# Two of six triangular inverses move to GpSimd, VectorE's work in PSUM, and a new order for the planned part

## The chip, the cores and the metric

The kernel runs on one core of one Trainium2 chip. The metric is device time in microseconds (us) of one execution; the kernel before takes 930.67 us, the median of three runs (928.48 to 932.31). A profile of a single execution is read beside it.

## The reference, cut to what matters

Three layers follow each other. The first is a delta-rule attention over 32 heads (4 batches of 8), 768 steps, head size 48; the second sends each of the 3072 tokens to one of 8 experts; the third is a dense layer with SiLU.

```
for t in range(768):                       # every head
    y[t]  = q[t] @ state
    state = state + beta[t] * outer(k_n[t], v[t] - k_n[t] @ state)
e   = argmax(x @ w_gate + bias[modality])   # x = y, 384 wide
out = gate * (relu(x @ w1[e]) @ w2[e])      # hidden 1024
h   = out @ w_in;  y = (h * sigmoid(h)) @ w_out   # hidden 2048
```

All data are float32. The kernel works on the attention in chunks: within 128 steps the recurrence becomes a lower triangular system, whose inverse is needed before the chunk can touch the state.

## The kernel before, in words

The sequence is cut into six tiles of 128 steps, numbered 0 to 5, each in two halves p of the heads. For one tile TensorE makes Gram matrices of the keys (`gram`, job "gr") and of queries with keys ("gq"); ScalarE copies them to the array `G`, and VectorE masks the second kind into `KB` (`keep_reads`, job "Kc", L347). VectorE turns the 32x32 diagonal blocks into lanes (`to_lanes`, "L", L361), works out scales (`scales`, "b2", L373 to L383), and inverts all of them at once in 31 steps (`step`, "st"): step j scales eight columns of `L` now and then (L399), and adds to the columns right of j of the array `A`, for j under 3 with one instruction a row (L403), later with a product into `tmp` (L416) and a sum into `A` (L422), each split in even and odd rows. `spread` ("sp", L438) turns `A` back into `G`. From there TensorE joins blocks ("px", "pt", "po"), weighs keys ("w"), and goes through the states ("up", "ps", "py"), ScalarE copying every result out of PSUM. Tile t+1's states wait for tile t's. `lengthen` ("ln", L388) and `values` ("va") feed the values.

After tiles 1, 2, 4 and 5 a routing piece ("wv") picks experts for the tokens at hand and makes lists of rows ("idx"). GpSimd gathers rows by these lists ("xg"). Nine expert slots follow: five of 256 tokens (slots 0 to 4), whose work stands in the same plan as the attention, and four of 512 tokens, written as a loop (`regular`). A slot has eight chunks; for each chunk TensorE multiplies nine float32r products ("fi", L1252) and, in the five small slots, two plain float32 products ("se", L1346, four records in a trace). The dense layer follows with six groups of 512 tokens, and its weights are prepared (`Parts64`) on VectorE and ScalarE while the experts run.

What sets the order. `Attention.plan` and `Experts.plan` hand about 1700 jobs with an engine, a cost and predecessors to `Order.solve`, a list scheduler that picks among ready jobs by a rank (a table of numbers, `PLAN["rank"]`, minus the length of the tail). `Order.emit` then writes all jobs in order of planned start, and ties each engine's instructions in that order. So every engine works strictly in its planned order, and each of its waits holds back all that is behind it. Where TensorE has a planned gap of over 0.35 us, `pulses` puts in products of ones with ones (L709, 512 columns), whose results nobody reads; after 0.9 us of gap a pulse waits for the last VectorE or ScalarE job that the plan has just finished. They stop at the time at which the first list of rows is planned to be ready.

Of the kernel before, what the change touches and what calls it, by code (L numbers as in the profile page):

```python
# [7 lines left out]
F32 = mybir.dt.float32  # L8
# [14 lines left out]
    one=3, pair=(),  # L23
    rank=dict(
        kq=198.9, qb=242.4, vs=64.9, kd=1074.8, gr=178.8, gq=-206.4, Gc=265.8, Kc=-543.5, dg=116.5, zero=481.9,
        L=-45.2, sc=-154.7, b2=340.1, ln=213.1, va=184.7, st=-507.6, sp=-287.4, ga=-146.4, px=174.1, pt=-1057.9,
        X=305.7, T=-753.7, po=227.7, o=-75.7, w=-47.4, wc=358.3, up=-972, uc=248.6, ps=313.7, sc2=440.7, py=-130,
        Y=295.3, out=42.8, xt=584.3, xc=262.8, gt=-535.2, wv1=331.6, wv2=-1257.8, wv4=-528.6, wv5=1423.9, one=13,
        kz=-116.7, ask=630.4, gates=494.4, val=-1272.9, fe=560.9, xg=-121.2, tr=351.3, th=-1084.9, tl=-543.8,
        s1h=188.5, s1l=-470.8, fi=62.6, rh=1130.9, se=363.3, ev=879.6, ys=-330, kq0=-992.8, kq1=204, kq2=-239,  # L30
        kq3=1181.7, kq4=1140.9, kq5=361.6, qb0=-834.3, qb1=213, qb2=198.2, qb3=-423.8, qb4=-77.2, qb5=-59.4,
        vs0=275.8, vs1=225.8, vs2=298.3, vs3=263.5, vs4=296.8, vs5=998, kd0=157.9, kd1=428.8, kd2=-1243.7,
        kd3=-217.5, kd4=145.9, kd5=155.3, gr0=-340.2, gr1=-583.9, gr2=-34.8, gr3=329.1, gr4=454.4, gr5=93.2,
        gq0=-633.4, gq1=162.2, gq2=-384.1, gq3=-361, gq4=1032.9, gq5=1017.3, Gc0=235.9, Gc1=-709.5, Gc2=429.7,
        Gc3=314.6, Gc4=-129.9, Gc5=270.9, Kc0=-373, Kc1=999.8, Kc2=144.2, Kc3=-455.6, Kc4=155, Kc5=266.9, dg0=-223.6,
        dg1=-1210.5, dg2=1184.8, dg3=-248, dg4=-20.1, dg5=-606.1, zero0=116.4, zero1=332.4, zero2=1460.5,
        zero3=248.9, zero4=333.9, zero5=159.4, L0=447.7, L1=-430.7, L2=924.8, L3=192.6, L4=921.1, L5=183, sc0=1012.1,
        sc1=-98.1, sc3=224.1, sc4=1211.5, sc5=-69.1, b20=922.8, b21=538.7, b22=973.6, b23=880.2, b24=185.3,
        b25=1234.7, ln0=-63.4, ln1=1192.8, ln2=1025.7, ln3=125.5, ln4=-1285.8, ln5=-18.4, va0=-105.9, va1=173.4,
        va2=-105.7, va3=542.3, va4=-431.2, va5=-166.7, st0=-382.7, st1=226.4, st2=409.7, st3=238.7, st4=991.3,  # L40
        st5=297.4, sp0=1026.6, sp1=-1254, sp2=258.7, sp3=-652.1, sp4=319.6, sp5=-558.9, ga0=216.1, ga1=274.9,
        ga2=-353.3, ga3=81.8, ga4=378.1, ga5=-391.6, px0=-256, px1=-219.1, px2=-501.3, px3=228.8, px4=-782.7,
        px5=-706.1, pt0=1186.1, pt1=1, pt2=1002.2, pt3=-69.1, pt4=137.4, pt5=540.7, X0=154.8, X1=-283.2, X2=143.5,
        X3=223.1, X4=167.8, X5=355.1, T0=-942.6, T1=-981.1, T2=559.4, T3=375.1, T4=290.1, T5=-757.6, po0=-44.5,
        po1=-483.3, po2=37.4, po3=453.9, po4=173.6, po5=7.6, o0=547.1, o1=1388.5, o2=-397.4, o3=-1124.1, o4=-93.5,
        o5=1261.4, w0=607.9, w1=-55.3, w2=250.4, w3=-492.5, w4=338.1, w5=-29.2, wc0=441.5, wc1=204.1, wc2=-303.8,
        wc3=303.5, wc4=18.8, wc5=-839.4, up0=307.4, up1=961.3, up2=997.7, up3=151.7, up4=276.1, up5=165.9, uc0=71.2,
        uc1=7.9, uc2=168.8, uc3=400.9, uc4=-365.6, uc5=-21.5, ps0=-362, ps1=192.1, ps2=-98.2, ps3=-284.9,
        ps4=-1201.7, ps5=388.1, sc20=-17.9, sc21=-203.8, sc22=1135, sc23=1058.3, sc24=266, sc25=262.1, py0=-1236.1,
        py1=-1483.9, py2=178.4, py3=159.7, py4=157.6, py5=260.2, Y0=-591.1, Y1=106.6, Y2=225.6, Y3=173.9, Y4=-364.7,  # L50
        Y5=581.7, out0=1102.9, out1=219.8, out2=-5, out3=1095, out4=106.6, out5=7.9, xt0=-110.6, xt1=1262.9,
        xt2=-77.8, xt3=558.1, xt4=320.5, xt5=-355.9, xc0=-1176.7, xc1=446.2, xc2=190.5, xc3=1185.8, xc4=-1224.2,
        xc5=-108.2, gt0=-51.7, gt1=446.3, gt2=320.9, gt3=-396.2, gt4=195.5, gt5=988.7,
    ), half=82.5,
    ex=300.9, n0=40, npre=40, tok=70,
# [3 lines left out]
class Order:  # L59
# [1803 lines left out]
```

## Time and profile before

| | us |
|---|---|
| device time, median of 3 (lowest, highest) | 930.67 (928.48, 932.31) |
| profiled execution, device time | 937.53 |
| profiled execution, span | 935.8 |
| TensorE busy | 887.8 (95%) |
| VectorE busy | 587.1 (63%) |
| ScalarE busy | 424.6 (45%) |
| GpSimd busy | 80.9 (9%) |
| mean granted TensorE clock | 0.97 of full speed |

The profiled execution takes 6.9 us more than the median of the runs, and its span is 1.7 us shorter than its own device time. TensorE's busy time holds the idle products and counts a product from its start to its modelled end, so it isn't work at the peak. The span has three parts: the planned part up to the last eviction of slot 4, the four large expert slots, and the dense layer. Names of tiles in the rows are the program's: `KKQ` and `KRH` are keys, `bank` the five PSUM banks of the plan, `po` two further ones that hold the experts' sums, `raw` the expert weights as fetched, `wRH` and `pairs` their split halves, `raw_...` in evictions the rows to be scattered.

### The profile page before, as it was taken

How to read it: one execution, taken by the hardware profiler on the slowest of the kernel's cores; microseconds unless marked ns; L12 is line 12 of the kernel's file. 1: busy time of each engine (PE TensorE's matmuls, PEld its weight loads, DVE VectorE, ACT ScalarE, POOL GpSimd, SP SyncE). 2: the span in 40 equal slices, each digit the busy share in tenths (PEclk: the TensorE clock that was granted, in tenths of full speed). 3: DMA queues.
4: the chain of work that ended last, by engine and by line, in shares of the span. 5: the costliest groups of instructions: out<-in, count | busy, mean ns of one | idle time of the engine just before them, and what ended most of it. 6: DMA issues, size and time to landing. Idle time of an engine off the chain costs nothing. (4 is left out here: it accounts for less than half of the span.)

```text
span 935.8 us, 23105 instructions
## 1 busy us (share of the span) xinstructions
PE 887.8 (95%) x9293; PEld 739.7 (79%) x9293; DVE 587.1 (63%) x1671; ACT 424.6 (45%) x832; POOL 80.9 (9%) x85
## 2 busy tenths in 40 slices
PE   7779998978999899999999999999999999999998
PEld 4448888776888677888997888888888888888897
DVE  4999998989943594599973676543443443343332
ACT  4228566854687533456653544332332233233232
POOL 5000000010001135122211000000000000000000
PEclk8899989987999999999999999999999999999999
DMA  8933745636154504666652631030030100100100
GB/s 202 177 103 98 168 104 145 153 89 204 26 130 126 184 26 127 199 204 217 199 191 54 115 71 52 10 54 5 13 55 1 21 15 1 23 11 1 30 6 34
DMA packets 135350, 85.27 MB, mean 91 GB/s; under 512 B 102361, under 2 KB 121447, under 8 KB 135232
## 3 DMA queue, kind: packets, MB, share of 16 engines
q1 hardware_dynamic: 131904, 73.84, 32.0%
q0 software_dynamic: 3328, 9.83, 3.1%
q8 instruction: 76, 1.25, 0.6%
q14 instruction: 42, 0.34, 0.1%
HBM read 70.53 MB, written 14.55 MB: 91 GB/s over the span
## 5 line engine op out<-in xcount | busy, mean ns | idle before, releaser
L1655 PE MATMUL fpo<-fgh,o 128*128 128x512 f32 x480 | 162.8, 396 | 0.0
L1646 DVE TENSOR_TENSOR fq<-fy,fgh 128x512 fp32r<-128x512 f32 x96 | 66.1, 689 | 110.7 <-ACT fgh L1644 103.9
L1642 DVE TENSOR_TENSOR fy<-fph,fy 128x512 f32<-128x512 f32 x96 | 66.2, 690 | 110.3 <-ACT fy L1640 110.0
L1644 ACT CAST fgh<-fy 128x512 fp32r<-128x512 f32 x96 | 59.6, 621 | 130.7 <-PE fpo L1655 99.1
L1640 ACT ACTIVATE fy<-fph 128x512 f32<-128x512 f32 x96 | 57.5, 599 | 124.0 <-PE fph L1637 122.2
L1637 PE MATMUL fph<-fxh,il 128*128 128x512 f32 x288 | 113.2, 393 | 0.0
L1637 PE MATMUL fph<-fxh,ih 128*128 128x512 f32 x288 | 113.1, 393 | 0.0
L1655 PEld LDWEIGHTS fpo<-fgh,o 128*128 128x128 f32 x480 | 90.2, 188 | 21.3
L1655 PE MATMUL fpo<-fq,o 128*128 128x512 f32 x240 | 95.0, 396 | 0.0
L1259 PE MATMUL poe<-w2s,pairs 128*128 128x384 f32 x384 | 75.6, 339 | 0.0
L416 DVE TENSOR_TENSOR tmp<-A,L 128x126 f32<-128x126 f32 (+20 forms) x336 | 70.6, 251 | 0.9
L1259 PEld LDWEIGHTS poe<-w2s,pairs 128*128 128x128 f32 x384 | 68.1, 188 | 3.7 <-DVE w2s L1216 0.2
L422 DVE TENSOR_TENSOR A<-A,tmp 128x126 f32<-128x126 f32 (+20 forms) x336 | 70.3, 250 | 0.0
L1252 PE MATMUL bank<-xh,wRH 128*128 128x256 f32 x240 | 62.2, 336 | 4.2 <-DVE wRH L1308 3.7
L1637 PEld LDWEIGHTS fph<-fxh,il 128*128 128x128 f32 x288 | 54.1, 188 | 12.0
L1637 PEld LDWEIGHTS fph<-fxh,ih 128*128 128x128 f32 x288 | 54.1, 188 | 12.0
L1346 PE MATMUL po<-raw,hs 128*128 128x384 f32 x160 | 62.3, 514 | 0.0
L1637 PE MATMUL fph<-fq,ih 128*128 128x512 f32 x144 | 56.9, 395 | 0.0
L1637 PE MATMUL fph<-fxl,ih 128*128 128x512 f32 x144 | 56.3, 391 | 0.0
L1655 PEld LDWEIGHTS fpo<-fq,o 128*128 128x128 f32 x240 | 45.1, 188 | 10.9
L1252 PEld LDWEIGHTS bank<-xh,wRH 128*128 128x128 f32 x240 | 42.3, 202 | 9.4 <-DVE wRH L1308 4.1
L709 PE MATMUL po<-ones 128*128 128x512 bf16 x103 | 34.0, 446 | 13.7 <-DVE KB L347 5.4
(436 smaller groups left out, 1661.4 us busy)
## 6 DMA issues: line engine op xcount, KB each, us to landing
raw<-in_moe_w_dram SPq DMA_DIRECT2D x72, 384.0 KB
ri<-in_moe_w_in_dram SPq DMA_DIRECT2D x12, 512.0 KB
ro<-in_moe_w_out_dram SPq DMA_DIRECT2D x16, 384.0 KB
vs<-in_vd_dram SPq DMA_DIRECT2D x12, 384.0 KB
KI<-in_kd_dram SPq DMA_DIRECT2D x24, 192.0 KB
Z<-vs SPq DMA_DIRECT2D x24, 192.0 KB
xs<-Y SPq DMA_DIRECT2D x48, 96.0 KB
fy<-ys SPq DMA_DIRECT2D x72, 64.0 KB
```

What stands on the lines that cost most here:

```text
L416: nc.vector.tensor_tensor(tv, r[:, :, j : j + 1].to_broadcast([128, c, n]), L[:, j : j + 1, j + 1 :].to_broadcast([128, c, n]), op=ALU.mult,)
L422: nc.vector.tensor_tensor(r[:, :, j + 1 :], r[:, :, j + 1 :], tv, op=ALU.add)
L709: return nc.tensor.matmul(room, dense, dense[:, None, :].to_broadcast([128, 4, 128]), start=True, stop=True).ins
L1252: self.nc.tensor.matmul(ph, a[:, k, :], b[:, k, :], start=(i == 0), stop=(i == 8))
L1259: self.mark = self.nc.tensor.matmul(o, a[:, cs], b, start=(c == 0 and i == 0), stop=(c == self.F - 1 and i == 2)).ins
L1346: nc.tensor.matmul(self.po[b][:, 0:384], v["h"][c % 2][:, 128 * b : 128 * b + 128], self.raw(1, c), start=(c == 0), stop=(c == F - 1),)
L1637: nc.tensor.matmul(ph, a[:, k, fs], b[:, k, :], start=(n == 0), stop=(n == 8))
L1640: nc.scalar.activation(sg, ph, AF.Sigmoid)
L1642: nc.vector.tensor_tensor(gv, ph, sg, op=ALU.mult)
L1644: self.marks = [nc.scalar.copy(gh, gv).ins]
L1646: self.marks.append(nc.vector.tensor_tensor(gl, gv, gh, op=ALU.subtract).ins)
L1655: nc.tensor.matmul(po[k], a[:, rows], b, start=(f == 0 and i == 0), stop=(f == 15 and i == 2))
```

## The change

The inverses of tiles 1 and 4 run on GpSimd ("p" in `lanes`), those of tiles 0, 2, 3 and 5 on VectorE ("v"). The recursion goes by rows now: step j takes row j of the inverse, multiplies it by a column of `L`, and adds it to all rows below. GpSimd has its array `A` in SBUF and does a step in two instructions. VectorE's array lies in the two PSUM banks `po`, even rows in one and odd rows in the other, and a step takes four instructions; TensorE clears these banks with products of zeros (`nil`), and `spread` takes two transposes there.

The idle products are halved in size, come in pairs, write another bank, stand in all planned gaps of the plan, and wait only for jobs that the next real work of TensorE needs anyway. Slots 3 and 4 (`passes`) split the second expert weight and the hidden rows in high and low float32r parts, and take three products a block in place of one float32 product. The constants of the router are made in pieces ("ci" on GpSimd, "cc" on VectorE), one after another, between other jobs. In the large slots, VectorE takes every second eviction. The rank table, most of the planned costs of TensorE's jobs, and so the whole order are new.

```diff
-    one=3, pair=(),
+    lanes="vpvvpv", passes=(3, 4),
     rank=dict(
-        kq=198.9, qb=242.4, vs=64.9, kd=1074.8, gr=178.8, gq=-206.4, Gc=265.8, Kc=-543.5, dg=116.5, zero=481.9,
+        kq=8.3, qb=131.9, vs=96.2, kd=87.8, gr=66.6, gq=88.5, Gc=-5.7, Kc=-272, dg=53.6, zero=-520, L=7.4, sc=-311.2,
...
     def clear_inverses(self, t):
-        A = self.st[t]["A"] = self.pools["ln"].tile([128, 32, 32], F32, tag="A", name=f"A{t}", bufs=2)
-        self.nc.gpsimd.memset(A, 0.0)
+        if PLAN["lanes"][t] == "p":
+            A = self.st[t]["A"] = self.pools["ln"].tile([128, 32, 32], F32, tag="A", name=f"A{t}")
+            self.nc.gpsimd.memset(A, 0.0)
+            return
+        self.st[t]["A"] = self.rows
+        for x in self.rows:
+            self.nc.tensor.matmul(
+                x, self.nil, self.dense[:, None, :].to_broadcast([128, 4, 128]), start=True, stop=True
+            )
...
     def step(self, t, j):
+        L, A = self.st[t]["L"], self.st[t]["A"]
+        pool = PLAN["lanes"][t] == "p"
+        eng = self.nc.gpsimd if pool else self.nc.vector
         if j % 8 == 0:
+            ls = L[:, j : j + 8]
+            eng.tensor_tensor(ls, ls, self.st[t]["b2"][:, None, :].to_broadcast([128, 8, 32]), op=ALU.mult)
+        c = j + 1
+        if pool:
+            parts = [(A[:, c:, 0:c], A[:, j : j + 1, 0:c], L[:, j, c:, None])]
+        else:
+            row = A[j % 2][:, j // 2 : j // 2 + 1, 0:c]
+            parts = []
+            for w in (c % 2, j % 2):
+                k = (c + 1 - w) // 2
+                if k < 16:
+                    parts.append((A[w][:, k:, 0:c], row, L[:, j, 2 * k + w :: 2, None]))
...
+            tv = tmp[:, : n * c].rearrange("p (a b) -> p a b", b=c)
+            eng.tensor_tensor(tv, row.to_broadcast([128, n, c]), l.to_broadcast([128, n, c]), op=ALU.mult)
             tmps.append(tv)
+        for (x, _, _), tv in zip(parts, tmps):
+            eng.tensor_tensor(x, x, tv, op=ALU.add)
...
+        for j, (count, cast) in enumerate(router.consts):
+            once(("ci", j), "POOL", 0.25, 0, count, [("cc", j - 1) if j else ("b2", 0)])
+            once(("cc", j), "DVE", 0.25, 0, cast, [("ci", j)])
...
+        def relu_low(s, c):
+            hh, hl = v["hh"][c % 2], v["hh"][2 + c % 2]
+            nc.vector.scalar_tensor_tensor(hl, v["ph", s, c], 0.0, hh, op0=ALU.max, op1=ALU.subtract)
...
-            nc.scalar.mul(ysb, po[t], g["gate"][:, o : o + 1])
+            if t % 2:
+                nc.vector.tensor_scalar(ysb, po[t], g["gate"][:, o : o + 1], None, op0=ALU.mult)
+            else:
+                nc.scalar.mul(ysb, po[t], g["gate"][:, o : o + 1])
```

The order changes at these places. First, VectorE up to the first turning into lanes, before:

```order
L742 CAST lane<-lanei 128x128 [waits Pool_49]
L742 CAST k_136<-k128i 128x24 [waits Pool_49]
L353 COPY G<-G 32x512 [waits Activation_49]
L742 CAST k_140<-k256i 128x12 [waits Pool_49]
L742 CAST slot<-sloti 128x52 [waits Pool_49]
L742 CAST down<-downi 128x8 [waits Pool_49]
L742 CAST ti<-tii 128x24 [waits Pool_49]
L752 CAST V<-ti 128x24 [waits DVE_49]
L742 CAST pi<-pii 128x24 [waits Pool_49]
L754 CAST V<-pi 128x24 [waits DVE_49]
L353 COPY G<-G 32x512 [waits Activation_49]
L361 STREAM_TRANSPOSE L_309<-G 128x1024 [waits DVE_49,Activation_49]
```

And the same place now:

```order
L371 COPY G<-G 32x512 [waits Activation_49] x2
L391 STREAM_TRANSPOSE L_322<-G 128x1024 [waits DVE_49,Activation_49]
L828 MEMSET wg 128x96
L365 TENSOR_TENSOR KB_102<-bank_126,amask 64x512 [waits PE_49,Pool_49]
L365 TENSOR_TENSOR KB_102<-bank_126,amask 64x512 [waits Pool_49]
L365 TENSOR_TENSOR KB_102<-bank_124,amask 64x512 [waits PE_49]
L365 TENSOR_TENSOR KB_102<-bank_124,amask 64x512
L403 RECIPROCAL rn_427<-n_0_369 128x32 [waits Activation_49]
```

The casts of the router's constants stood ahead of the second copy in `G` and of the first turning; now both copies come first, and four rows of `KB` (eight before) lie between the turning and the scales. In all, 24 rows of `KB` stood between the first turning and the spread of tile 0; now there are eight, and 16 come behind that spread.

Second, GpSimd in the inverse of tile 1 (`A_171` its array, the arrays `k128i` and `k256i` constants of the router); before, GpSimd stood here:

```order
L357 MEMSET A_329 128x1024 [waits Pool_49]
L357 MEMSET A_333 128x1024
L740 IOTA k256i 128x12 [waits DVE_49]
L740 IOTA sloti 128x52 [waits DVE_49]
L740 IOTA downi 128x8 [waits DVE_49]
L740 IOTA tii 128x24 [waits DVE_49]
L740 IOTA pii 128x24 [waits DVE_49]
L357 MEMSET A_910 128x1024 [waits DVE_49]
```

And now, from step 19 of the 31 on:

```order
L456 TENSOR_TENSOR A_171<-A_171,tmp_19_0_952 128x12x20 [waits Pool_49]
L789 IOTA k128i 128x24 [waits DVE_49]
L453 TENSOR_TENSOR tmp_20_0_995<-A_171,L_489 128x231 [waits Pool_49]
L456 TENSOR_TENSOR A_171<-A_171,tmp_20_0_995 128x11x21 [waits Pool_49]
L453 TENSOR_TENSOR tmp_21_0_1032<-A_171,L_489 128x220 [waits Pool_49]
L456 TENSOR_TENSOR A_171<-A_171,tmp_21_0_1032 128x10x22 [waits Pool_49]
L453 TENSOR_TENSOR tmp_22_0_1057<-A_171,L_489 128x207 [waits Pool_49]
L456 TENSOR_TENSOR A_171<-A_171,tmp_22_0_1057 128x9x23 [waits Pool_49]
L789 IOTA k256i 128x12 [waits DVE_49]
```

Each of the 62 products and sums waits for the one before it on the same engine, and six of the seven constants stand between steps 19 and 30, each waiting for VectorE's cast of the one before.

Third, VectorE around the spread of tile 1, before (`A_333` is tile 1's array, `L_1615` tile 2 in lanes):

```order
L422 TENSOR_TENSOR A_333<-A_333,tmp_30_0_1574 128x16 [waits DVE_49]
L422 TENSOR_TENSOR A_333<-A_333,tmp_30_1_1576 128x15 [waits DVE_49]
L438 STREAM_TRANSPOSE G<-A_333 128x32x32 [waits DVE_49]
L361 STREAM_TRANSPOSE L_1615<-G 128x1024 [waits DMAHW4_49,DMAHW1_49,DMAHW5_49,DMAHW0_49,Activation_49]
L388 TENSOR_TENSOR vs_0_716<-vs_0_716,nt_1003 128x768
L388 TENSOR_TENSOR vs_1_834<-vs_1_834,nt_1003 128x768 [waits DMAHW7_49]
```

And now (`A_171` is tile 1's array, `L_1320` tile 2 in lanes):

```order
L423 TENSOR_TENSOR vs_1_854<-vs_1_854,nt_568 128x768 [waits DMAHW5_49]
L791 CAST V<-pii 128x24 [waits Pool_49]
L391 STREAM_TRANSPOSE L_1320<-G 128x1024 [waits DMAHW4_49,DMAHW1_49,DMAHW5_49,DMAHW0_49,Activation_49]
L468 STREAM_TRANSPOSE G<-A_171 128x32x32 [waits Pool_49]
L403 RECIPROCAL rn_1438<-n_2_1381 128x32 [waits Activation_49]
L404 SCALAR_TENSOR_TENSOR rn_1438<-L_1320,rn_1438 128x32 [waits DVE_49]
```

The spread of tile 1 waits for GpSimd now, and tile 2's scales and inverse on VectorE stand behind that wait. Tile 4's spread waits for GpSimd in the same way, ahead of tile 5's inverse, and GpSimd's first gather of rows stands behind the last step of tile 4.

## Rows read from the trace of the kernel before

**Rows 1.** Windows: length; busy us of PE, PEld, DVE, ACT, POOL (instructions); clock.
```profile
0.00:64.50 64.50, 47.17 (x713) 27.05 (x713) 50.41 (x177) 16.11 (x24) 13.12 (x28) 0.87 0.80 174
64.50:169.80 105.30, 97.44 (x2897) 89.83 (x2898) 98.14 (x425) 72.42 (x153) 2.86 (x3) 0.95 0.49 121
169.80:264.50 94.70, 84.21 (x1896) 72.25 (x1893) 86.42 (x386) 59.09 (x126) 5.24 (x5) 0.91 0.45 115
264.50:387.40 122.90, 117.49 (x1295) 93.89 (x1296) 64.32 (x181) 65.44 (x149) 30.88 (x23) 0.97 0.42 124
387.40:935.80 548.40, 541.50 (x2498) 456.64 (x2495) 287.84 (x504) 211.53 (x383) 28.82 (x26) 0.99 0.25 64
```

**Rows 2.** Timeline (start, us): spreads of tiles 0 and 5, slot 4's last eviction.
```profile
62.46 2.02 DVE L438 STREAM_TRANSPOSE G<-A 128x1024 f32<-128x1024 f32 x1
...
262.36 2.12 DVE L438 STREAM_TRANSPOSE G<-A 128x1024 f32<-128x1024 f32 x1
...
386.83 1.23 ACT L1352 ACTIVATE raw<-po,gate 128x384 f32<-128x384 f32 x2 [0.34 <-PE po L1346]
```

**Rows 3.** Timeline, end of tile 0's second diagonal copy, and the first turning.
```profile
9.75 0.62 ACT L353 COPY G<-G 32x512 f32<-32x512 f32 x1
...
16.08 1.92 DVE L361 STREAM_TRANSPOSE L<-G 128x1024 f32<-128x1024 f32 x1
```

**Rows 4.** Groups of VectorE, 16 to 64.5 us: instructions, busy us, mean ns, idle.
```profile
L347 DVE TENSOR_TENSOR KB<-bank,amask 64x512 f32<-64x512 f32 x24 | 16.5, 687 | 0.5
...
L388 DVE TENSOR_TENSOR vs<-vs,nt 128x768 f32<-128x768 f32 x2 | 1.9, 958 | 0.1
```

**Rows 5.** Timeline of VectorE, tile 1's inverse: start, one step's products, spread.
```profile
70.08 0.20 DVE L383 TENSOR_SCALAR A<-b 128x32 f32<-128x32 f32 x1
...
73.38 0.40 DVE L416 TENSOR_TENSOR tmp<-A,L 128x100 f32<-128x100 f32 x2
...
92.07 2.05 DVE L438 STREAM_TRANSPOSE G<-A 128x1024 f32<-128x1024 f32 x1
```

**Rows 6.** Groups of VectorE: both inputs in SBUF, one in PSUM, output in PSUM.
```profile
L1308 DVE TENSOR_TENSOR wRH<-raw,wRH 128x384 fp32r<-128x384 f32 x40 | 21.8, 553 | 28.8 <-ACT wRH L1305 26.8 <-PE bank L1252 1.8
...
L1335 DVE TENSOR_TENSOR xl<-bank,xh 128x384 fp32r<-128x384 f32 x10 | 5.2, 548 | 10.6 <-DMA Z<-vs 6.3 <-ACT xh L1333 4.4
...
L1618 DVE STREAM_TRANSPOSE fpt<-fy 128x512 f32<-128x512 f32 x3 | 2.2, 721 | 3.7 <-DMA fy<-ys 3.6
```

**Rows 7.** Groups of GpSimd in the first 60 us.
```profile
L357 POOL MEMSET A<- 128x1024 f32 x2 | 1.8, 947 | 0.0
...
L291 POOL TENSOR_SCALAR_AFFINE_SELECT amask<-amask 64x64 f32<-64x64 f32 x2 | 0.7, 346 | 0.0
masks.py:199 POOL TENSOR_SCALAR_AFFINE_SELECT ident<-ident 128x128 f32<-128x128 f32 x1 | 0.3, 294 | 0.1
...
masks.py:197 POOL MEMSET ident<- 128x128 f32 x1 | 0.2, 205 | 0.3 <-POOLq L1845 0.3
```

**Rows 8.** Group of the idle products on TensorE, whole planned part.
```profile
L709 PE MATMUL po<-ones 128*128 128x512 bf16 x103 | 34.0, 446 | 13.7 <-DVE KB L347 5.4 <-DVE A L422 4.0 <-POOL ones L762 1.6
```

**Rows 9.** Timeline of TensorE in slot 3 and in a large slot.
```profile
356.94 1.46 PE L1346 MATMUL po<-raw,hs 128*128 128x384 f32 x4
...
359.31 1.46 PE L1346 MATMUL po<-raw,hs 128*128 128x384 f32 x4
...
442.19 1.58 PE L1259 MATMUL poe<-w2s,pairs 128*128 128x384 f32 x8
443.61 0.86 PE L1252 MATMUL ph<-pairs,wRH 128*128 128x512 f32 x3
```

**Rows 10.** Timeline of GpSimd's gathers: one beside busy VectorE, one after.
```profile
329.18 3.58 POOL L1220 DMA_INDIRECT xg<-xs,gidx  x1 [0.30 <-issue]
...
355.95 0.99 POOL L1220 DMA_INDIRECT xg<-xs,gidx  x1 [1.02 <-DVE scratch L1117]
```

More of the change, by code (lines that the diff above doesn't have):

```diff
@@ L163, in solve, with ahead, pulses @@
         return self.line
-    def pulses(self, until):
+    def ahead(self, j):
+        if not hasattr(self, "former"):
+            self.former, last = {}, {}
+            for x in self.line:
+                self.former[x["key"]] = last.get(x["e"])
+                last[x["e"]] = x["key"]
+        jobs, seen, todo = self.jobs, set(), [k for k in j["after"] if k in self.ids]
+        while todo:
+            k = todo.pop()
+            if k is None or k in seen:
+                continue
+            seen.add(k)
+            todo += [x for x in jobs[self.ids[k]]["after"] if x in self.ids] + [self.former[k]]
+        return seen
+    def pulses(self):
         line, out, at = [j for j in self.line if j["e"] == "PE"], [], 0.0
@@ L169, in pulses @@
         for j in line:
-            if at > until:
-                break
             if j["start"] - at > 0.35:
+                safe, first = self.ahead(j), at == 0.0
                 x = max(at + 0.02, j["start"] - 9.0)
-                while x + 0.3 < j["start"]:
-                    behind = [n for end, n in others if x - 1.2 < end <= x - 0.1] if x - at > 0.9 else []
+                while x + (1.5 if first else 0.3) < j["start"]:
+                    behind = []
+                    if x - at > 0.9 and not first:
+                        behind = [n for end, n in others if x - 1.2 < end <= x - 0.1 and n in safe]
                     out.append((x, behind[-1] if behind else None))
@@ L254, in __init__ @@
             nc.vector.memset(self.halves[32 * q : 32 * q + 32, q % 2 : q % 2 + 1], 1.0)
+        self.nil = cp.tile([128, 128], BF16, name="nil")
+        nc.vector.memset(self.nil, 0.0)
         self.bl = cp.tile([128, T, 32], F32, name="bl")
@@ L686, in wave @@
         half = self.T // 2
-        needs = [("gt", t, 3)]
+        needs = [("gt", t, 3), ("tris",)] + [("cc", j) for j in range(len(router.consts))]
         if t % half == half - 1:
@@ L1277, in open @@
             b["h1"], b["l1"] = ([rest(x, 128) for x in ws[k : k + 2]] for k in (0, 2))
+        if what == "p":
+            self.v["hh"] = cut(ar.tile([128, 1024], F32R, tag="KQ1", name="hhl"), [256] * 4)
         if what == "o":
@@ L1356, in before @@
             return [(name, k // F, k % F, b)] if 0 <= k < F * S else []
+        done = [("gt", T - 1, 3)] + [("out", T - 1, p, e) for p in range(2) for e in range(2)]
         for s in range(S + 1):
```

268 lines of the change are left out of this document (137 added, 131 removed).

## The prediction

> **What bounds the kernel now.** I first cut the span into stages where the attention hands on its result, and read the windows of each; then the timeline at the cuts, and then the groups inside. The stages end with the spread of tile 0 at 64.5 us, of tile 3 at 169.8, of tile 5 at 264.5, and with the last eviction of slot 4 at 386.83 + 1.23 = 388.1 [rows 1, 2]. Behind that lie 548.4 us of large slots and dense layer, in which TensorE is busy for 541.5 [rows 1]. In the first three stages VectorE is busy for 50.4 + 98.1 + 86.4 = 234.9 of 264.5 us. TensorE shows 47.2 + 97.4 + 84.2 there, which looks as full; but 34.0 us of it, over the planned part, are 103 idle products [rows 8], and it cannot join a tile's blocks before VectorE has spread that tile. So up to 264.5 us the chain runs through VectorE's inverses. After it VectorE is half idle (64.3 of 122.9 us) and TensorE is the bound (117.5 of 122.9) [rows 1]. The question is how far VectorE can be relieved before TensorE takes over.
>
> **Step 1, the start.** The second diagonal copy of tile 0 ends at 10.37 us, and the first turning starts only at 16.08 [rows 3]: between them stand the casts of the router's constants, in the order of before. They go. Two loads of queries now stand ahead of keys, for which I leave about 2 us: the turning starts at 12.3, a gain of 3.8. Of the 24 rows of `KB` before tile 0's spread 16 move behind it: 24 x 687 ns are 16.5 us busy, and as neighbours overlap a little I take 0.70 us each, 11.2 us. The two L388 (1.9 us) move too [rows 4]. Tile 1's scales come in, 1.8 us, which I size by L388's pair. The spread in PSUM is two transposes of 512 elements; the nearest row has 721 ns [rows 6] against 2.02 for one of 1024 in SBUF [rows 2], a gain of 0.6. Sum: 3.8 + 11.2 + 1.9 - 1.8 + 0.6 = 15.7, so tile 0 is spread at 64.5 - 15.7 = 48.8.
>
> **Step 2, an inverse of VectorE in PSUM.** Tile 1's takes from 70.08 to 92.07, 22.0 us [rows 5]. By rows it has 126 instructions against 118 and about as many elements. Inputs from PSUM cost nothing that shows: 548 ns against 553 for two inputs in SBUF [rows 6]. I take 22.0 + 0.3. The trace has no chain of dependent instructions inside PSUM. If each of some 122 hops were 0.1 us dearer, an inverse would cost 34; if each step gained what [rows 6] show, 5 ns of 553, it would stay near 22; 21 is the low end if the products (a step's pair takes 0.40 us [rows 5]) gained a twentieth. I stay by the row of equal sizes.
>
> **Step 3, an inverse on GpSimd.** 62 dependent instructions and four scalings, with 2 x 5456 = 10,912 elements per partition. No row shows a GpSimd product of two arrays. The memsets give a slope of (947 - 205)/896 = 0.83 ns an element written and, from 205 ns for 128, about 0.10 us fixed; one stream read adds (294 - 205)/128 = 0.70 [rows 7]. Two streams read: 0.83 + 2 x 0.70 = 2.23 ns. So 62 x 0.15 (fixed, and 0.05 for the hop) = 9.3, 10,912 x 2.23 = 24.3, the scalings (1024 elements) 2.9: about 37 us. At the memset's rate alone it would be 17; at the 346 ns of a 64 x 64 select, 5.4 ns an element if all of it were slope, 74 [rows 7]. I take 37, built on the rows with slopes.
>
> The Trainium skill ("GPSIMD Engine Reference", § 3.1 Elementwise — side-by-side cycle accounting) puts a GpSimd element at about 2.6 cycles where VectorE takes one. No run here shows it; by its measured sum of 2048 elements, 4497 ns, the elements would cost about 24 us, an estimate that leaves the forecast where it is.
>
> GpSimd starts when tile 1's scales are there, about 26.6 us (12.3, then turning and scales of both tiles and the first steps), and is done at 64. VectorE reaches tile 1's spread only after tile 0's spread, tile 2's rows and scales, 16 rows of `KB` (11.2), copies, casts and the L388: 48.8 + 22 = 70.8. So the wait is covered by 7 us, which is gone once the GpSimd inverse takes over about 45; beyond that every us moves tile 2's scales and inverse, which stand behind the waiting spread, and all after them. Tile 1 is spread at about 73 (before 94.1 [rows 5]).
>
> **Step 4, TensorE between the spreads.** In the order of before 1475 small products stand between the joins of tiles 0 and 3, and TensorE is busy for 97.4 us in that stretch [rows 1]: 0.066 us each, idle products included. In the new order 352, 492, 666, 444 and 491 stand between the joins of tiles 0 to 5, 2445 in all (before 533, 390, 552, 545, 326), with two expert chunks instead of seven. A chunk of slot 3 takes 359.31 - 356.94 = 2.37 us [rows 9]. From 48.8, with 2 us for the join: 50.8 + 2445 x 0.066 + 2 x 2.37 = 217. VectorE by itself: busy 184.6 us from 64.5 to 264.5 [rows 1], less two inverses (44.0), plus the 16 rows (11.2) and casts and copies (4.5), with 8 us of waits, 164; 48.8 + 164 = 213. TensorE is a little later; with fewer idle products I take 216 for the spread of tile 5, 48.5 us earlier. Most of what VectorE gives up is thus real, and the rest is capped by TensorE.
>
> **Step 5, the last planned stage.** It was 122.9 us. Five chunks that stood before it now stand in it: 5 x 2.37 = 11.9. In slots 3 and 4 two plain products become six float32r ones: eight of a large slot take 443.61 - 442.19 = 1.42, 0.177 each, so six take 1.06; the old four records are busy for 1.46, of which the eight's own overlap (1.58 - 1.42 = 0.16) is to be taken: 1.30 [rows 9]. 16 chunks x 0.24 = 3.9 saved. The extra splits cost VectorE at most 16 x 2 x 0.55 = 17.6 us (548 ns for 384 columns [rows 6], these have fewer), in a stage where it has 58 us free. 122.9 + 11.9 - 3.9 = 130.9, so slot 4 ends at 347, 41 us before 388.
>
> **Step 6, the rest.** In the large slots half the evictions move from ScalarE to VectorE. They have TensorE's 541.5 of 548.4 us as cover [rows 1]; I take 0, and 3 if VectorE delays the chunks. The halved idle products fill waits; if the clock (granted mean 0.87, 0.95, 0.91, 0.97 by stage [rows 1]) falls further in the shorter chain, TensorE's stages pay, some 5 us for 0.03 of 165.
>
> Sum against the profiled execution (span 935.8, device 937.5): 937.5 - 41 = 896.5. That execution is 6.9 us above the median of the runs; the same 41 off the median gives **889 us**.
>
> **Rivals.**
> A port shared by VectorE and GpSimd. A gather on GpSimd took 3.58 us beside a busy VectorE and 0.99 when it was not [rows 10]: 2.6 us lost to company. VectorE's rows in PSUM leave it few instructions with two SBUF inputs during GpSimd's inverses: about 12 in tile 1's, which its slack hides, and about 25 in tile 4's; with 0.3 us for each, the mean of such a product and its wait, 8 us come in, and the time is 897. Chance 0.19. The Trainium skill ("SBUF — State Buffer", Who interferes with whom) states such a rule: a VectorE instruction with two SBUF inputs contends with a GpSimd one that reads SBUF, as an exclusive lock, and one with at most one SBUF input does not; by that rule, the gathers in the trace agree, but don't separate it from a late list of rows.
>
> GpSimd as the bound (slower). If its inverse costs d, over about 47 us both tile 1 and tile 4 come late and VectorE stands behind them: 2 x (d - 47). That eats the 41 us at d = 68. At 74, the upper bound of step 3, it is 54 us, so 889 + 54 = 943. For it speaks that no row shows the operation and that six of the router's constants, each waiting for a cast on VectorE, stand between its last steps; against it the two slopes, which give half of that. Chance 0.08.
>
> Hops in PSUM. At 0.1 us each, four inverses cost 4 x 12 = 48 more, less some 15 that TensorE's lateness hides: 889 + 33 = 922. Against it the equal rows of step 2. Chance 0.05.
>
> The order does not hold: real waits, strung in a fixed order, return 15 to 25 us, or the numbers of jobs hide stalls that I could not see from the old trace: 905 to 914. The change then does half of what it says. Chance 0.08.
>
> **How the numbers follow.** 0.60 for the forecast, whose own range is 875 to 902; the others as given. The range, from 866 (TensorE at 0.060 a product, GpSimd free) to 926 (hops in PSUM, or GpSimd at 65), leaves out GpSimd's tail and a start that is much better. About 0.5%, 4.7 us, is what the runs can tell from no change. Faster by more than that: the forecast, the port, and of the hops and the half order (0.13) all but 0.04, which goes to no change: 0.60 + 0.19 + 0.09 = 0.88. Slower is GpSimd's case, 0.08.
>
> **What would show it.** The spread of tile 1 should start at about 71 us, and wait for VectorE's own work, not for GpSimd; GpSimd's products and sums should average 0.55 us; VectorE's steps stay near 0.2 us. Tile 5's spread should stand at 214 to 217, slot 4's last eviction near 347, and a large slot's chunk should take what it takes now. I am wrong if VectorE idles at tile 1's or tile 4's spread with GpSimd as its releaser, if the steps in PSUM are clearly longer, or if TensorE waits between the joins for more than 10% of the time.

## The result

The changed kernel takes 923.94 us (median of 20 runs, 920.18 to 932.91) against 932.59 of the kernel before beside it: ratio 0.991, 95% interval 0.989 to 0.993. One of the 20 runs of the kernel before took 2976 us; the ratio leaves it out as a slow one. Two later comparisons, on the chips of e9 and e16 below, gave 0.986 (0.982 to 0.989) and 0.987 (0.984 to 0.991). So the change saves 9 to 14 us, where 41 were forecast. The sign was right, the size was not, by a factor of three to five.

The profiled execution takes 931.4 us, 7.5 above the median, as that of before lies 6.9 above its own; its span is 929.7 us (before 935.8). Here are its windows, cut at the same events as [rows 1]: end of tile 0's spread, of tile 3's, of tile 5's, last eviction of slot 4. Columns as there, with PE clock, DMA share and GB/s at the end.

```profile
0.00:52.90 52.90, 38.37 (x591) 30.39 (x592) 39.52 (x166) 16.41 (x24) 31.71 (x58) 0.81 0.90 175
52.90:157.40 104.50, 97.91 (x2957) 90.74 (x2958) 92.57 (x342) 71.69 (x152) 33.79 (x64) 0.97 0.58 140
157.40:238.00 80.60, 75.14 (x1955) 69.17 (x1952) 66.63 (x259) 53.00 (x114) 28.33 (x44) 0.89 0.53 141
238.00:380.90 142.90, 133.42 (x1443) 112.03 (x1438) 99.43 (x261) 82.78 (x188) 29.27 (x24) 0.99 0.45 134
380.90:929.70 548.80, 539.98 (x2466) 455.23 (x2466) 272.11 (x469) 201.11 (x361) 30.98 (x26) 0.99 0.23 56
```

Stage by stage before, then after: 64.5 and 52.9; 105.3 and 104.5; 94.7 and 80.6; 122.9 and 142.9; 548.4 and 548.8. The third stage gains 14 us and the fourth gives 20 back; expert chunks have moved from the one into the other. What stays is the first stage. Now the same as one row each, from the end of tile 0's spread to slot 4's last eviction, first of before, then of the changed kernel:

```profile
64.50:388.10 323.60, 299.84 (x6096) 256.67 (x6097) 248.88 (x990) 197.55 (x427) 39.39 (x32) 0.95 0.45 120
```

```profile
52.90:380.90 328.00, 306.47 (x6339) 271.94 (x6338) 258.63 (x858) 207.47 (x454) 91.40 (x131) 0.96 0.51 138
```

That is the whole result: 323.6 and 328.0. Behind tile 0's spread the planned part takes as long as before (323.4 and 322.5 us in two later profiles of the changed kernel, e9 and e16), with TensorE busy for 93% of it in both rows. The earlier start, 11.5 us here and 14.8 and 13.8 in the two later profiles, is all there is. (VectorE isn't lighter either, 258.6 against 248.9: two inverses have left, but 16 rows of `KB`, the splits of slots 3 and 4 and dense weights, prepared earlier, have come in.)

The single steps, in VectorE's timeline: the spreads of tiles 0, 1 and 5 [rows 2, 5], with what stands before them, and ScalarE's last evictions of slot 4.

```profile
51.04 1.95 DVE L471 STREAM_TRANSPOSE G<-po 128x512 f32<-128x512 f32 x2
...
74.01 1.96 DVE L391 STREAM_TRANSPOSE L<-G 128x1024 f32<-128x1024 f32 x1
75.89 1.92 DVE L468 STREAM_TRANSPOSE G<-A 128x1024 f32<-128x1024 f32 x1
...
236.06 1.98 DVE L471 STREAM_TRANSPOSE G<-po 128x512 f32<-128x512 f32 x2
...
379.80 1.05 ACT L1411 ACTIVATE raw<-po,gate 128x384 f32<-128x384 f32 x2
```

Tile 1's spread follows VectorE's own turning without a gap: it doesn't wait for GpSimd, whose last sum there ended 1.6 us earlier (ahead of that turning, VectorE's cast of a router constant waited 0.7 us for GpSimd):

```profile
74.06 0.25 POOL L456 TENSOR_TENSOR A<-A,tmp 128x31 f32<-128x31 f32 x1
```

GpSimd's groups, whole span: 62 products and 62 sums in the two inverses, which took 44.2 us (from 30.07) and 43.6 (from 140.84).

```profile
L453 POOL TENSOR_TENSOR tmp<-A,L 128x31 f32<-128x31 f32 (+15 forms) x62 | 36.1, 583 | 4.4
L456 POOL TENSOR_TENSOR A<-A,tmp 128x31 f32<-128x31 f32 (+15 forms) x62 | 34.8, 561 | 4.9
```

### The profile page after: what moved, and what is told of

It reads as the page before. It is cut to its first block, busy times and chain, and to the rows that moved or that the text cites. A ratio compares the mean times of both kernels' runs of the same rounds, so it can differ in the third digit from the quotient of the medians.

```text
span 929.7 us, 23254 instructions
## 1 busy us (share of the span) xinstructions
PE 884.8 (95%) x9396; PEld 757.6 (81%) x9396; DVE 570.3 (61%) x1490; ACT 425.0 (46%) x838; POOL 154.1 (17%) x213
## 5 line engine op out<-in xcount | busy, mean ns | idle before, releaser
L1723 PEld LDWEIGHTS fpo<-fgh,o 128*128 128x128 f32 x480 | 90.3, 188 | 21.5
L1299 PE MATMUL bank<-xh,wRH 128*128 128x256 f32 x240 | 56.7, 313 | 3.4 <-DVE wRH L1357 3.1
L1267 POOL DMA_INDIRECT xg<-xs,gidx x26 | 30.8, 1183 | 127.5 <-PE bank L1281 89.5
L456 DVE TENSOR_TENSOR po<-po,tmp 128x126 f32<-128x126 f32 (+35 forms) x244 | 50.0, 250 | 0.1
L453 DVE TENSOR_TENSOR tmp<-po,L 128x126 f32<-128x126 f32 (+35 forms) x244 | 49.2, 242 | 0.7
L1299 PEld LDWEIGHTS bank<-xh,wRH 128*128 128x128 f32 x240 | 40.2, 192 | 9.7 <-DVE wRH L1357 4.2
L1299 PE MATMUL ph<-pairs,wRH 128*128 128x512 f32 x144 | 39.0, 411 | 3.7 <-DVEq L1558 3.7
```

The costliest lines, as they stand in the source:

```text
L453: eng.tensor_tensor(tv, row.to_broadcast([128, n, c]), l.to_broadcast([128, n, c]), op=ALU.mult)
L456: eng.tensor_tensor(x, x, tv, op=ALU.add)
L1267: self.nc.gpsimd.indirect_dma_start(out=rows, out_offset=None, in_=self.xs[0 : self.xs.shape[0] // (2 - n), :], in_offset=bass.IndirectOff ...
L1299: self.nc.tensor.matmul(ph, a[:, k, :], b[:, k, :], start=(i == 0), stop=(i == 8))
L1723: nc.tensor.matmul(po[k], a[:, rows], b, start=(f == 0 and i == 0), stop=(f == 15 and i == 2))
```

## The experiments

Theory A: TensorE's own work is the floor behind tile 0's spread, and relief of VectorE is worth little there. Theory B: the forecast gain was real, and is lost where VectorE and GpSimd work side by side. Times are medians, with the ratio to the kernel before on the same chip and its 95% interval. The kernels of e1 to e3, e6, e15 and e17 leave out steps that the result needs; they are for timing alone. The edits are cut to what matters.

**Less inverse.** In `step`, with the order kept:

```diff
+        if t == 4 and 0 < j < 30:              # e1, e15, e17 (changed kernel)
+        if t in (1, 4) and 0 < j < 30:         # e2 (kernel before)
+        if True and 0 < j < 30:                # e3 (changed kernel)
+            return
```

e1: 

> The changed kernel in the same order, with steps 1 to 29 of tile 4's inverse on GpSimd left out, so that GpSimd is silent between 141 and 184 us. Theory A (TensorE has little left to wait for, so relief of VectorE is worth little): VectorE's small routing instructions become short, 0.2 us in place of 0.4 to 0.7, but tile 5's spread comes at most 4 us earlier than 235.8 and slot 4's last eviction at most 3 us before 380. Theory B (the forecast gain was there and is lost to VectorE and GpSimd slowing each other in the routing piece, which then costs TensorE its clock): VectorE's stretch from 159 to 182 us shrinks by 7 us or more, the granted clock from 157 to 199 us stays above 0.9 (0.79 now), tile 5's spread comes 8 to 15 us earlier and slot 4 ends 8 to 15 us earlier.

e2: 

> The kernel before in its own order, with steps 1 to 29 of the inverses of tiles 1 and 4 left out: VectorE gets 2 x 21 us back at no price at all, the best that a move of them to another engine could give without a new order. The prediction's steps 3 and 4: slot 4 ends some 30 to 40 us before 388. Theory A (TensorE's own work is the floor): TensorE waited or idled for only some 30 us between tile 0's spread and the end of slot 4, and has few of them in these two inverses, so slot 4 ends 8 to 18 us earlier.

e3: 

> The changed kernel in its order with steps 1 to 29 of all six inverses left out, on both engines. It shows the floor that everything else sets. Theory A: slot 4 still ends at 345 us or later, since 64 us at most of TensorE's 381 are idle or idle products, and 34 of them lie ahead of tile 0's spread, where some 22 of them go. Theory B: VectorE is what holds the planned part; slot 4 ends at 330 us or earlier.

e2 took 929.9 us, ratio 0.995 (0.991 to 0.998): with 41 us of VectorE taken away at no price, the kernel before gains 5 to 7 us. In its profile, of its fastest run, slot 4 ends 11.4 us earlier, inside A's 8 to 18 and far from the prediction's 30 to 40; 9.0 of these are TensorE's busy time (290.80 for 299.84), at a granted clock of 0.98 for 0.95. e3 took 910.2, ratio 0.972 (0.969 to 0.976). Their stretches from tile 0's spread to slot 4's end, in one row each:

```profile
64.40:376.70 312.30, 290.80 (x6095) 248.83 (x6096) 207.71 (x759) 197.24 (x427) 40.12 (x32) 0.98 0.47 125
```

```profile
32.80:361.30 328.50, 306.72 (x6381) 271.60 (x6378) 189.03 (x501) 207.12 (x454) 37.41 (x42) 0.98 0.55 146
```

In e3 VectorE is busy for 189 us in place of 259 and GpSimd for 37 in place of 91, and the stretch is 328.5 us, the same as with all six inverses. Slot 4 ends 19.5 us earlier, about as far as tile 0's spread is earlier (20.1). Theory A holds on this side; B's 330 us for slot 4's end is missed by 31.

e1 took 916.5 us, ratio 0.979 (0.975 to 0.982): more than A allowed. Slot 4 ends 12 us earlier than in the changed kernel's first profile (4 earlier than in the two later ones), 318.1 us after tile 0's spread. So something is lost beside GpSimd as well. VectorE's timeline in the routing piece (`choose`), first of the changed kernel, then of e1; the same instructions in the same order:

```profile
159.55 0.65 DVE L912 TENSOR_TENSOR eq<-lg,mx 128x64 f32<-128x64 f32 x1
160.12 0.21 DVE L913 TENSOR_TENSOR df<-lg,mx 128x64 f32<-128x64 f32 x1
160.26 0.70 DVE L914 TENSOR_TENSOR eq<-eq,down 128x64 f32<-128x64 f32 x1
160.99 0.22 DVE L916 TENSOR_REDUCE m<-eq 128x8 f32<-128x64 f32 x1
...
161.69 0.68 DVE L920 COPY ca<-OH 128x64 bf16<-128x64 bf16 x1
...
163.97 0.64 DVE L926 COPY cb<-ca 128x32 bf16<-128x32 bf16 x1
```

```profile
156.13 0.22 DVE L916 TENSOR_TENSOR eq<-lg,mx 128x64 f32<-128x64 f32 x1
156.27 0.22 DVE L917 TENSOR_TENSOR df<-lg,mx 128x64 f32<-128x64 f32 x1
156.40 0.22 DVE L918 TENSOR_TENSOR eq<-eq,down 128x64 f32<-128x64 f32 x1
156.66 0.22 DVE L920 TENSOR_REDUCE m<-eq 128x8 f32<-128x64 f32 x1
...
157.97 0.17 DVE L930 COPY cb<-ca 128x32 bf16<-128x32 bf16 x1
```

In these rows products and copies take 0.64 to 0.70 us beside GpSimd (`df`, right behind a slowed `eq`, 0.21) and 0.17 to 0.22 alone; the reduction, with one input, takes 0.22 in both. The 55 instructions of the first two routing pieces add up to 17.3 us in the changed kernel (17.2 and 16.2 in two later profiles), 10.6 in the kernel before and 10.6 in e1. TensorE waits at the end of that chain, and then its clock falls. Its row at the wait (the count of tokens), and its windows (us busy, clock, DMA share, GB/s), changed kernel first, then e1:

```profile
165.59 0.21 PE L936 MATMUL ranks<-cb,ones 128*128 128x64 bf16 x1 [2.06 <-DVE cb L930]
```

```profile
157.00:164.00 7.00, 6.48 (x186) 1.00 0.74 156
164.00:176.00 12.00, 9.82 (x185) 0.72 0.73 190
176.00:191.00 15.00, 14.16 (x314) 0.66 0.05 12
```

```profile
158.00:170.00 12.00, 11.41 (x347) 1.00 0.76 196
170.00:185.00 15.00, 14.44 (x469) 1.00 0.10 24
```

At a granted clock of 0.66 (0.5 is 1.2 GHz, 1.0 is 2.4 GHz) TensorE gets 314 products done in 15 us, at 1.0 469; the two stretches don't hold quite the same products. e1 has a fall of its own ahead of these windows, 0.76 from 151 to 158 us; over the whole stage its clock is 0.95 against 0.79.

**What the company costs.** The first comparison was across chips, so e1 was run again, alone and then beside the changed kernel itself (e16).

e15: 

> The run without steps 1 to 29 of tile 4's inverse on GpSimd once more, beside the others. If what the company costs in time is real, it is 7 to 12 us faster than the changed kernel, 0.972 to 0.982 of the kernel before; with a ratio over 0.985 the first was a matter of the chip.

e16: 

> The changed kernel a third time, as the neighbour of the next run on one chip: 0.985 to 0.992 of the kernel before.

e17: 

> The changed kernel without steps 1 to 29 of tile 4's inverse on GpSimd, beside the changed kernel itself. If the company costs what the profiles show (VectorE's surplus of 6.7 us and a clock of 0.79 for a stretch of 41 us): 5 to 10 us faster than its neighbour. If TensorE makes up for it later: less than 3 us.

e15 took 917.3 us, ratio 0.986 (0.982 to 0.989), over the bound that it had set: by that, the size of e1's gain was a matter of the chip. On one chip e16 took 923.2, 0.987 (0.984 to 0.991), and e17 917.5, 0.982 (0.979 to 0.985). By this one pair the company costs 5.8 us, at the low end of the 5 to 10 expected; the six runs of each overlap a little (919.7 to 927.1 and 915.9 to 922.6). It is real, then, and far from the missing 27 to 32.

**Which company.** Two other forms of GpSimd's work in tile 4: halves of the rows (e5), and memsets in place of the steps (e6).

```diff
+            cuts = [c, (c + 33) // 2, 32] if t == 4 and c < 31 else [c, 32]      # e5
+            parts = [(A[:, x:y, 0:c], A[:, j : j + 1, 0:c], L[:, j, x:y, None]) for x, y in zip(cuts, cuts[1:])]
...
+        if t == 4 and 0 < j < 30:                                                 # e6
+            m = -(-23 * (31 - j) * (j + 1) // 320)
+            for _ in range(2):
+                self.nc.gpsimd.memset(self.st[t]["A"][:, 1 : 1 + m], 0.0)
+            return
```

e5: 

> The changed kernel in its order, with every product and sum of tile 4's steps on GpSimd cut into two halves of the rows. Theory E (a VectorE instruction that meets a GpSimd one waits for the end of it): the instructions of the routing piece between 157 and 184 us that took 0.4 to 0.7 us (0.2 without company) lose about half of their surplus, 3 to 4 us in all, GpSimd ends some 8 us later than 184, still ahead of the spread, and the whole gains 2 to 5 us. Theory F (they are slowed by GpSimd's work as such, in proportion): the surplus stays, and the whole is the same or up to 3 us slower.

e6: 

> The changed kernel in its order; steps 1 to 29 of tile 4 on GpSimd are two memsets each of about the same duration, which read nothing (tile 4's inverse is left out by that). Theory G (the surplus comes from two readers of SBUF): VectorE's routing instructions are as short as in the run without the steps, and slot 4 ends near 369. Theory H (any company of GpSimd costs, writing too): the surplus stays for at least the copies and casts, and slot 4 ends near 376 or later.

e5 took 918.4 us, ratio 0.988 (0.985 to 0.990). The 55 instructions add up to 15.1 us, and many of them take about half of the surplus; its row for the `eq` that took 0.65:

```profile
154.87 0.37 DVE L916 TENSOR_TENSOR eq<-lg,mx 128x64 f32<-128x64 f32 x1
```

So the delay goes with the length of the GpSimd instruction that is met, as theory E has it; the surplus lost is 2.2 us (about 3 in later runs with halves), where 3 to 4 were expected, and GpSimd ended at 184.3 us, some 6 later than in e4 and e8, still ahead of the spread. The time shows no gain: by its ratio e5 is no faster than the changed kernel (0.986 to 0.991). e6 took 920.5, ratio 0.988 (0.984 to 0.992), slot 4 ended at 374 us, between G's 369 and H's 376, and 13.5 us were left for the 55. Its timeline:

```profile
156.69 0.23 DVE L917 TENSOR_TENSOR eq<-lg,mx 128x64 f32<-128x64 f32 x1
156.97 0.22 DVE L919 TENSOR_TENSOR eq<-eq,down 128x64 f32<-128x64 f32 x1
...
157.73 0.35 DVE L925 COPY ca<-OH 128x64 bf16<-128x64 bf16 x1
158.11 0.59 DVE L931 COPY cb<-ca 128x8 bf16<-128x8 bf16 x1
158.74 0.57 DVE L931 COPY ca<-cb 128x16 bf16<-128x16 bf16 x1
```

Beside a GpSimd that only writes, these products with two SBUF inputs are as short as alone, and the copies are not (the small sums right behind the copies take about 0.5 us too; they end with the copy before them, so their own part can't be told). G is right for the products, H for the copies. This is the rule of the Trainium skill ("SBUF — State Buffer", Who interferes with whom): two SBUF inputs contend with GpSimd's reads and not with its writes, copies and casts can run in a mode that takes both ports and then contend in either case, reductions never do. The prediction said of any instruction with at most one SBUF input that it doesn't contend, and left that mode out: the copies have one input and were slowed.

**TensorE's clock and idle products.**

```diff
+                if j["key"] in (("wv", 1, "count"), ("wv", 2, "count")):   # e8, in emit
+                    for _ in range(4):
+                        pulse()
...
     def pulses(self):
+        return []                                                           # e7
```

e7: 

> The changed kernel without any idle product on TensorE. If they earn their place: the granted clock falls at and after tile 0's spread (0.81 up to 53 us and 1.0 from there now), the stages up to tile 3's spread take 5 to 15 us more, and the whole is 5 to 15 us slower. If the gaps are too short or too early to matter: within 3 us.

e8: 

> The changed kernel in its order, with eight more idle products ahead of each of the two countings of the routing piece (at 163 and 177 us), for which TensorE waits 2.4 and 1.1 us. Theory I (the clock's fall from 164 to 191 us follows on TensorE's waiting there, and costs about half of its 27 us of half speed in part): the granted clock from 157 to 199 us rises from 0.79 to above 0.9, tile 5's spread and slot 4's end come 4 to 9 us earlier. Theory J (VectorE's chain holds that stretch, the clock is only seen beside it): the clock may rise, but the spread of tile 4 stays within 2 us and the whole within 3 us.

e7 took 928.4 us, ratio 0.998 (0.996 to 1.000): the idle products are worth some 7 us (e8 on the same chip: 921.7; 6 to 11 by the ratios of the changed kernel). They work in the first stages, where the clock is 0.71 up to 55 us and 0.79 in the next 29 without them (0.81 and 1.00 with them). e8 took 921.7, ratio 0.990 (0.986 to 0.994). Two later profiles of the unchanged program, e9 and e16, settle it with e8's, one row each from 151 to 190 us in this order:

```profile
151.00:190.00 39.00, 35.55 (x837) 32.83 (x836) 30.66 (x100) 19.76 (x42) 23.42 (x40) 0.78 0.33 82
151.00:190.00 39.00, 33.89 (x948) 31.17 (x949) 32.05 (x104) 21.66 (x47) 26.89 (x44) 0.91 0.46 111
151.00:190.00 39.00, 35.37 (x948) 33.05 (x947) 31.23 (x101) 22.09 (x47) 26.11 (x42) 0.91 0.37 93
```

The clock is 0.78, 0.91 and 0.91; tile 4's spread begins at 188.8, 189.0 and 188.0 us, and slot 4 ends at 373.1, 373.2 and 370.7. That is J's case: the clock is seen beside the delay, and moves neither the spread by 2 us nor the end by 3.

**The three passes.**

```diff
         o.solve()
+        PLAN["passes"] = ()      # e4: jobs "rl", "s2h", "s2l" issue nothing then
```

e4: 

> The changed kernel in the same order, but slots 3 and 4 again with two plain products a chunk, without the splits of the second weight and of the hidden rows. Theory C (VectorE, full from 300 to 380 us, holds these slots up): the chunks of slots 3 and 4 take less time, slot 4 ends 3 to 8 us earlier and the whole is faster by as much. Theory D (the prediction's step 5: three passes save TensorE 0.24 us a chunk and VectorE has room): slot 4 ends 3 to 5 us later.

It took 925.6 us, ratio 0.988 (0.985 to 0.992), the same as the changed kernel. Its last stage:

```profile
232.40:374.04 141.64, 136.07 (x1403) 108.16 (x1399) 94.10 (x243) 78.70 (x177) 34.97 (x24) 0.99 0.45 139
```

It is 1.3 us shorter, with 5 us less of VectorE. Neither C's 3 to 8 us nor D's loss: without the passes TensorE is busy for 2.7 us more, and without an instruction for 3.9 less (5.6 for 9.5). In the changed kernel 2.3 us of TensorE's waits there end with VectorE's split of the hidden rows (`hhl`); e4 has none of these. So VectorE's splits take back what the passes save TensorE.

**Putting them together.** e9 is the changed kernel, e10 to e12 its combinations with halves, no passes and fill.

e9: 

> The changed kernel itself, on the chip of the three runs beside it, with a second profile. By all theories 0.988 to 0.994 of the kernel before. If its first profile was a typical one, the time from the end of tile 0's spread to slot 4's last eviction is 326 to 330 us again; if the company of GpSimd and the clock make it scatter, it lies between 318 and 326.

e10: 

> The changed kernel with tile 4's steps on GpSimd in halves, and without the three passes in slots 3 and 4. If both gains were real and lie on TensorE's path (3 us from the halves, 2 from the passes by the runs so far): 4 to 6 us faster than the changed kernel beside it. If the passes are worth what the prediction gave them: 1 us faster at most.

e11: 

> The changed kernel with the halves and with the idle products ahead of the two countings. In the run with halves alone the clock stayed at 1.00 from 152 to 188 us, so nothing is left for the fill: the same as halves alone, 2 to 5 us faster than the changed kernel. If the halves' clock was a lucky profile: 1 to 3 us better than halves alone.

e12: 

> Halves, no passes, and fill together: 4 to 7 us faster than the changed kernel beside it if the three add up; no better than the halves alone if TensorE's own work is all that is left.

On one chip: 921.7, 922.8, 922.4 and 920.5 us; ratios 0.986, 0.985, 0.985 and 0.983, each with an interval of 0.003 to 0.004 either way. e9 lies just below its expected 0.988, e10 and e11 gain nothing, and e12 gains 1.2 us where the three were to add up to 4 to 7: nothing here clearly beats the changed kernel. e9's stretch behind tile 0's spread:

```profile
49.70:373.10 323.40, 303.33 (x6339) 269.74 (x6338) 258.55 (x857) 207.29 (x454) 90.40 (x131) 0.97 0.51 140
```

So the first profile's 328.0 was on the long side.

**Slack or level?** What was open was whether VectorE has room behind tile 0's spread, and whether the gain is the start's alone.

```diff
+            for _ in range(2 if t in (2, 3, 5) else 1):                     # e13: each product twice
                 eng.tensor_tensor(tv, row.to_broadcast([128, n, c]), l.to_broadcast([128, n, c]), op=ALU.mult)
...
+        if (t, j) == (0, 30):                                               # e14: tile 0's spread late
+            for _ in range(10):
+                eng.tensor_tensor(L, L, L, op=ALU.mult)
```

e13: 

> The changed kernel in its order; VectorE makes every product of the steps of tiles 2, 3 and 5 twice, which adds about 61 x 0.19 = 11.6 us of VectorE to each of the three inverses, 35 us in all, behind tile 0's spread. Theory A in its strong form (behind tile 0's spread TensorE's own work is the floor and VectorE has slack): less than 8 us slower. Theory K (VectorE and TensorE bind in turns, TensorE takes over only when VectorE gets lighter): 20 to 35 us slower, though taking inverses away gains nearly nothing.

e14: 

> The changed kernel in its order, with ten dummy products of 128x1024 on VectorE just ahead of tile 0's spread, some 11 to 13 us. If the gain of the change is the earlier spread of tile 0 (about 13 us) and nothing behind it, slot 4 ends as much later as the spread comes later, and the time goes back to the kernel before within 4 us. If the gain was made behind the spread: the time rises by less than 5 us.

e13 took 969.2 us, ratio 1.042 (1.039 to 1.046). Its stretch from tile 0's spread to slot 4's end:

```profile
49.80:416.10 366.30, 313.06 (x6339) 276.23 (x6337) 300.15 (x1041) 207.93 (x454) 90.20 (x130) 0.92 0.46 123
```

VectorE's 41.5 us more (300.15 - 258.63) make the stretch 38 to 43 us longer (328.0 and 323.4 without). So theory A in its strong form falls, and K has the direction; the price is above its 20 to 35 us (34 to 43 by the spans of e13 and the first two profiles, about 50 by the ratios). Telling is the time in which TensorE has no instruction at all, length less busy time: 23.8 us in the row of before, 21.5 in that of the changed kernel, 21.5 in e2, 21.8 in e3 with no inverse left, and 53.2 in e13. Taking inverses from VectorE doesn't touch these 21 to 24 us, adding to them shows in full. The reading that fits, and that no single run shows, is that VectorE stands level with TensorE: their jobs lie in one chain through each tile, and whichever is later sets the pace.

e14 took 940.7 us, ratio 1.012 (1.007 to 1.017). Its ten dummy products took 15.6 us, not 11 to 13, and tile 0's spread began at 63.1 us, the place of before (62.5). From its end to slot 4's:

```profile
65.20:386.20 321.00, 299.57 (x6342) 265.50 (x6340) 258.24 (x858) 207.16 (x454) 86.65 (x124) 0.98 0.52 141
```

Slot 4 ended at 386.0, for 388.1 before, with a span of 934.0: by the profile the whole gain is gone, and the stretch is no longer than without the delay. By the medians it is 11 us slower than the kernel before, over the 4 that the expectation allowed; where these come from is open, as the profile is of one of its two fastest runs. So the gain is the start's, and behind it the changed kernel is no better than the kernel before. Which part of the change makes the start early no run separates; the inverse of tile 0 was on VectorE in both.

## Why the prediction was wrong

**What held.** Step 1: tile 0's spread was to end at 48.8 us; it ended at 53.0, and at 49.7 and 50.7 in two more profiles of the same program. Step 2: 22.3 us for an inverse in PSUM; tile 0's own step instructions took 22.2 from start to start, so PSUM has neither the dearer hops of the third rival nor a gain. Step 3: 37 us for GpSimd; 44 were measured, 583 and 561 ns an instruction where 550 was said, and the cover held by 1.6 us: no spread waited for GpSimd. The rival with GpSimd as the bound fell by that. Step 6: 548.8 us for 548.4.

**The step that failed is step 4**, "TensorE between the spreads". It gave TensorE 0.066 us a product and let the stage be the sum of them: 217 us for tile 5's spread, which came at 238. The rate was right; what failed is that the step had no term for waits. Here is TensorE from the end of tile 0's spread to that of tile 5's, and below it its idle products in that stretch:

```profile
52.90:238.00 185.10, 173.05 (x4904) 159.91 (x4905) 159.20 (x599) 124.69 (x266) 62.12 (x107) 0.94 0.56 140
```

```profile
52.90:238.00 185.10, 7.73 (x52) 4.34 (x52) 0.94 0.56 140
```

So 165.3 us are work, where the step had 166 (and 2 for a join); 7.7 are idle products, and 12.1 hold no instruction. 7.7 and 12.1 and a start 4.1 us late, less the 2 of the join and 0.8 of work, are the missing 21. Down to slot 4's end it is the same: 328.0 us are 297.6 of work (my numbers, 347 - 50.8, gave 296), 8.9 of idle products and 21.5 without an instruction.

The row of before had it. TensorE was busy for 97.44 + 84.21 + 117.49 = 299.1 of 322.9 us of these three stages [rows 1]. The step read 97.44 us as the duration and left out the 105.3 in which it was spent, though it gave VectorE 8 us of waits. Some 24 us without an instruction and 8.2 of idle products stood there, 32 in all, and the forecast took 25 of them (41 - 15.7) as if a chain in which engines hand each tile on ran without waits. e2 and e3 show that it keeps them. Had the stretch been kept at its 323.6 us and only step 1's 15.7 been taken, the forecast would have been 915.

The first paragraph had set TensorE's busy time aside for its 34.0 us of idle products; 25.8 of these lie ahead of tile 0's spread. And it had said "the chain runs through VectorE's inverses", from VectorE's 235 busy of 264 us. An engine that is busy for 89% of a stage is not alone its bound when another one is as full. e2 puts the number on it: 41 us of VectorE away, 5 to 7 us of time. The prediction's own sign of being wrong, waits of TensorE over 10% between the joins, did not catch it: 12.1 of 185.1 us are 6.5%, 10.7 with the idle products.

**Step 5** was mis-sized too: 142.9 us for a forecast 131. TensorE's busy time in the stage rose by 15.4 us (133.4, from 118.0 up to the eviction's end) where step 5 had 8.0, and its time without work by 4.1. Some 4 of the 7.4 are small products: 483 of them stand ahead of tile 0's spread (591 records less 108 idle products) where 640 had stood (713 less 73), and 99 more between the spreads (step 4), so 58 more come behind, an estimate at 0.066 us each. Another 1.2 are idle products, of which the stage had none before. The rest, some 2 us, is open; e3 and e4 show that neither the inverses nor the three passes made it. The passes' own term, 3.9 us for TensorE, was 2.7 by its busy time, and worth nothing in the time (e4).

**The port** had a chance of 0.19 and a price of 8 us. It came: 6.7 us of VectorE, 5.8 us of time. It is the smaller part of the miss. The larger part is the fourth rival, at a chance of 0.08: real waits in a fixed order were to return 15 to 25 us, and with the idle products about 30 came back (8.9 + 21.5), so the time lies above its 914. That 923.9 us lies inside the stated range of 866 to 926 is luck: its upper end was set by hops in PSUM or a GpSimd inverse of 65 us, and neither came.

## What to carry to other kernels

Before taking work off a busy engine, sum the busy time of the others over the same stretch, from the first hand-over to the last: what is free on the fullest of them, idle products counted as free, is about the most that can come back (busy time itself shrinks a little at a higher granted clock, as in e2), and waits that a chain of engines has now it may well keep: here they stayed at 21 to 24 us. Test it from both sides, since work left out may show nothing where the same work doubled shows its full price. And an engine that takes work over can slow its neighbour: here GpSimd cost VectorE 6.7 us on a chain of 55 small instructions, many of them copies or with two SBUF inputs.

## What the runs showed of the hardware

A short VectorE copy, or product with two SBUF inputs, that meets GpSimd waits for about one GpSimd instruction: 0.65 in place of 0.22 us beside products of 0.6 us, 0.37 beside halves. GpSimd can wait as well: its product of 128x87 at 180.75 us took 1.72 us beside a VectorE product of 1.93, and 0.33 at 32.36 us, when VectorE's inverse was in PSUM. A VectorE instruction with one input in PSUM pays nothing: the 122 products and sums of tile 0's inverse, most of them beside GpSimd, add up to 24.7 us, those of tile 5's, with GpSimd all but silent, to 24.9, and the rows of `KB` beside GpSimd take 0.69 us, as before.

After plain float32 products, the first float32r product of the next chunk takes 0.58 us in place of 0.28; it is where the old form of slots 3 and 4 lost TensorE's time, not in the four plain records, which advance by 0.99 us against 1.06 for the six. TensorE's timeline of the changed kernel in a plain slot, and in slot 4:

```profile
305.71 1.45 PE L1405 MATMUL po<-raw,hs 128*128 128x384 f32 x4
306.70 0.58 PE L1299 MATMUL bank<-xh,wRH 128*128 128x256 f32 x1
...
360.00 1.22 PE L1306 MATMUL po<-pairs,hhl 128*128 128x384 f32 x6
361.06 0.28 PE L1299 MATMUL bank<-xh,wRH 128*128 128x256 f32 x1
```
